# Thirteen clears of a scratch tensor move from SyncE's DMA queue to ScalarE's

## The chip, the core and the metric

The kernel runs on one core of a Trainium2 chip. The metric is device time in microseconds (us) of one execution. The engines of the core are named as in the profile: PE (TensorE, matmuls; PEld are its weight loads), DVE (VectorE), ACT (ScalarE), POOL (GpSimd) and SP (SyncE, which issues transfers here and computes nothing).

## The reference, cut to what matters

Three layers follow each other: attention in which a query sees only the keys of its own cluster, a mixture of eight experts that routes each token to one of them, and a gated feed-forward layer.

```python
q_assign = argmax(einsum('bhsd,hcd->bhsc', q_n, c_n), -1)      # 2 x 8 heads, 768 rows, 64 columns, 16 clusters
k_assign = argmax(einsum('bhsd,hcd->bhsc', k_n, c_n), -1)
mask = q_assign[:, :, :, None] == k_assign[:, :, None, :]
scores = where(mask, scale * q @ k.T, -1e9)
x = softmax(scores) @ v                                        # -> 1536 tokens x 512
expert_idx = argmax(x @ w_gate, axis=1)                        # 8 experts
disp[e, counts[e]] = x[i]                                      # token i to the next free row of its expert
y = relu(disp @ w1) @ w2;  out[i] = gate_w[i] * y[expert, pos] # 512 -> 1024 -> 512
h = out @ w_in;  result = (h * tanh(softplus(h))) @ w_out      # 512 -> 2048 -> 512
```

`disp` starts from zeros; rows that no token takes stay zero.

## The kernel before

The attention is one loop over 32 units (16 heads, two blocks of 384 queries each), each of three steps. In one step PE makes the scores of a pair of key tiles (`s`, L772 and L773), the product whose maximum is wanted (`pm`, L698) and a third of the product with the values (`pa`, L824). ACT takes the exponential (`P`, L780) and copies `pm` out of PSUM (`ev`, L707); DVE halves the copies to a maximum (L714, L718), writes it into the queries' tile (`QX`, L741), makes the low half of the probabilities (`PL`, L796) and normalizes (L847 to L863). The tiles `s`, `pm` and `pl` share a ring of three double banks in PSUM. Per head, `kf`, `qf` and `vf` are loaded (L413), split into high and low halves (`QK`, L528 to L537, copied to `KX` and `QX` at L541 or L544, on ACT or DVE), and turned by transposing transfers: `QKT` (L559), `KXT` and `QXT` (L664), and per unit `Q` (L745). Every one of these transfers is issued from SP.

The rows that the experts read lie in a scratch tensor `xs` in DRAM. It must hold zeros before tokens are written to it. `clear_xs` writes one thirteenth of it from a tile of zeros; the loop's callback `extra` calls it at steps 10, 12, ... 34. After each half of the heads the tokens are routed, and twelve indirect transfers on POOL (`dispatch`, L1171) write them into `xs`; these wait for all clears (`self.CLb`). The transposing transfers `xv` and `xt` (L1442) then read the experts' rows.

The order of all instructions comes from a planner. Each operation is added with an engine and an expected duration and is put into the first gap of that engine's plan in which its inputs are ready and the gap is long enough; `best` takes the engine on which an operation would end first, after a bias. At the end everything is emitted in the order of its planned time, and each engine executes its instructions in that order. Free gaps in PE's plan are filled with matmuls on zeros (L473, L477). For a transfer, `dma` books the issuing queue, a resource `HW` that both hardware queues share, and the transfer time:

```python
hold, hw, delay = (max(1175.0, 348 + xfer), 625, 900) if turn else (475, 450, 1125)
...
t1 = self._gap(q, t, hold)
t = self._gap("HW", t1, hw) if hw else t1
```

In the emitted program each transfer of the hardware queues counts up one of eight completion semaphores, which are taken in turn, and waits until the transfer eight places before it, the last user of that semaphore, has landed.

Of the kernel before, what the change touches and what calls it, by code (L numbers as in the profile page):

```python
# [277 lines left out]
class Builder:  # L278
# [86 lines left out]

    def clear_xs(self, xs, i, n):
        rows = xs.shape[0] // n
        self.nc.sync.dma_start(
            out=xs[i * rows:(i + 1) * rows].rearrange("(a p) c -> p a c", p=128),
            in_=self.zero16.unsqueeze(1).to_broadcast([128, rows // 128, self.RW]))  # L370

# [1809 lines left out]
    def run(self):  # L2181
        tc, nc, E, G, P = self.tc, self.nc, self.E, self.G, self.cfg
        NT, B, NB = self.NT, self.B, self.NB
        profile = [min(a, b) for a, b in zip(P["profile"], self.worst)]
        with ExitStack() as ctx:
            const = ctx.enter_context(tc.tile_pool(name="const", bufs=1))
            dram = ctx.enter_context(tc.tile_pool(name="dram", bufs=1, space=DRAM))
            small = self.small = ctx.enter_context(tc.tile_pool(name="small", bufs=1))
            rows = E * self.slots + max(self.va, default=0)
            xs = dram.tile([-(-rows // (128 * P["zn"])) * 128 * P["zn"], self.RW], F16, name="xs")  # L2190
            idc = dram.tile([self.N, 1], I32, name="idc")
            self.xsave = dram.tile([128, B, NT, 2 * self.KD, 128], F16, name="xsave")
            self.xs_views = dram_disjoint_views(xs[:, :], G)
            idc_views = dram_disjoint_views(idc[:, :], G)
            self.out_views = dram_disjoint_views(self.out, G)
            mkeep = const.tile([128, B * self.H * NB, 3], F32, name="mkeep")
            self.LG = const.tile([128, B, NT, E], F32, name="LG")
            self.OH = const.tile([128, G, E], F16, name="OH")
            self.CS = const.tile([128, B, E], F16, name="CS")
            self.POS = const.tile([128, G], F32, name="POS")  # L2200
            self.OVER = const.tile([128, G], F32, name="OVER")
            self.SLOT = const.tile([128, G], I32, name="SLOT")
            self.prof = const.tile([128, E], F32, name="prof")
            self.many = const.tile([128, B * self.H // self.EG], F32, name="many")
            self.buffers()
            plan = self.new_plan()
            right, actx, rctx, pctx = ExitStack(), ExitStack(), ExitStack(), ExitStack()
            xp = right.enter_context(tc.tile_pool(name="xp", bufs=1, side="right"))
            self.XD = [xp.tile([128, NT, self.XC, 128], F16, name="xd", tag="xd", bufs=B) for b in range(B)]
            self.chp = right.enter_context(tc.tile_pool(name="chp", bufs=1, side="right"))  # L2210

            self.PADb = Buf("pad", 1)

            def extra(z, now):
                k = z - P["zx"]
                if z in (6, 8):
                    pad = self.XD[(z - 6) // 2 % B][:, :, 2 * self.KD].bitcast(F32)
                    plan.op("POOL", 430, lambda: nc.gpsimd.memset(pad, 0.0), add=self.PADb, slack=now)
                if z == 4:
                    self.plan_gate_weights(plan, now)  # L2220
                step, n = P["zs"], P["zn"]
                if 0 <= k < step * n and k % step == 0:
                    assert not self.XSb.writers
                    plan.dma("SP", 22000 / n, lambda: self.clear_xs(xs, k // step, n), add=self.CLb, slack=now)
                if z == 56:
                    plan.dma("SP", 500, lambda: self.clear_idc(idc), new=self.IDCb, slack=now)

            def free(part):
                if part == 1:
                    wo = [xp.tile([128, NT, self.XC, 128], F16, name="xd", tag="xd", bufs=B).rearrange("p t c x -> p (t c x)") for b in range(B)]  # L2230
                    n = self.XC * NT * 128 // (2 * self.DM)
                    return [w[:, f * 2 * self.DM:(f + 1) * 2 * self.DM].rearrange("p (a c) -> p a c", a=2) for w in wo for f in range(n)]

            def before(part):
                if isinstance(part, int):
                    (actx, rctx, pctx)[part].close()
                    return
                use = [u for t in part for b in plan.rings.get(t, ()) for u in b.uses]
                return tuple(max(u[j] for u in use) for j in range(2))

            with tc.manual_schedule():
                self.constants(const, profile)
                self.attention(actx, rctx, pctx, plan, mkeep, extra, self.second_half(plan, profile, xs, idc, idc_views, before, free, mkeep))
                plan.emit()
            self.later.close()
            right.close()
            with tc.If(nc.values_load(self.flag[0:1, 0:1], min_val=0, max_val=1) > 0):
                self.general(mkeep, xs, idc, idc_views, small)
# [125 lines left out]
```

## Time and profile before

| | |
|---|---|
| time, median of 3 runs | 670.84 us (667.78, 670.84, 674.40) |
| profiled execution | 665.95 us |
| its span, first to last instruction | 664.2 us |
| mean granted TensorE clock | 0.99 of full speed |
| stretch in which the 13 clears are issued | 45.6 to 100.6 us |

The span is one execution, the slowest core's (there is one core). Busy times are sums of instruction durations; issues of transfers are not counted in them. A wait is put down to what released it last. "To landing" is the time from a transfer's issue to its completion.

### The profile page before, as it was taken

The page shows a single profiled execution, that of the slowest core. Times are in us where ns is not written, and L with a number is a line of the kernel's source. Part 1 is how long each engine was busy: PE and PEld are TensorE (multiplying, and loading weights), DVE is VectorE, ACT ScalarE, POOL GpSimd, SP SyncE. Part 2 cuts the span into 40 slices and gives each one's busy share as a digit, 9 for nine tenths or more (in the row PEclk, how much of TensorE's full clock was granted, in tenths as well). Part 3 has the DMA queues.
Part 4 walks back from the last instruction along what each step waited for, and adds up shares of the span by engine and source line. Part 5 has one row for each costly group of instructions (what it writes and reads, how often), then busy time and mean ns, then how long its engine had stood idle before and what let it go on. Part 6 is the DMA issues. An engine that isn't in the chain of part 4 may idle for free.

```text
span 664.2 us, 15345 instructions
## 1 busy us (share of the span) xinstructions
PE 626.3 (94%) x6100; PEld 450.7 (68%) x6100; DVE 542.7 (82%) x1047; ACT 487.1 (73%) x738; POOL 67.4 (10%) x113
## 2 busy tenths in 40 slices
PE   7999998799999998999999999979999999999993
PEld 5678776587787896789999886535555555555541
DVE  8999989989998857898899995999798788445542
ACT  6698897688887345576777766998988887666760
POOL 4000111110400030000000000000820000002203
PEclk9999999999998999999999999999999999999998
DMA  9879999894877879998889971213342221000102
GB/s 213 172 144 257 240 249 202 145 176 85 174 150 204 213 269 310 316 288 259 266 256 316 250 267 63 98 63 96 64 63 65 66 93 34 1 0 33 64 1 100
DMA packets 150322, 104.99 MB, mean 158 GB/s; under 512 B 92128, under 2 KB 133088, under 8 KB 150240
## 3 DMA queue, kind: packets, MB, share of 16 engines
q1 hardware_dynamic: 147936, 97.22, 58.8%
q0 software_dynamic: 2304, 6.69, 2.8%
q8 instruction: 50, 0.82, 0.6%
q14 instruction: 32, 0.26, 0.1%
HBM read 68.21 MB, written 14.36 MB: 124 GB/s over the span
## 4 chain that ended last, share of the span: by engine, by line
PE 53%; DVE 16%; DMA 9%; ACT 9%; issue 8%; SPq 2%; POOL 1%; DVEq 0%; POOLq 0%; ACTq 0%
PE fh L1933 13%; PE po L2021 12%; PE py L1648 6%; PE ph L1599 6%; PE pa L824 5%; DVE wh L1481 3%; DMA w2s<-in_moe_w_in_dram 2%; ACT P L780 2%; PE s L772 2%; DVE PL L796 2%; PE s L773 2%; DVE eh L714 2%; ACT ev L707 2%; PE pyv L1774 2%; PE pm L698 2%
## 5 line engine op out<-in xcount | busy, mean ns | idle before, releaser
L2021 PEld LDWEIGHTS <-gt 128*128 128x128 f16 x576 | 56.3, 98 | 64.9
L2021 PE MATMUL po<-xd,gt 128*128 128x512 f16 x432 | 97.3, 379 | 0.0
L780 ACT ACTIVATE P<-s 128x768 f32<-128x768 f32 x96 | 78.1, 814 | 22.1 <-PE s L773 21.5
L1648 PE MATMUL py<-ht,wh 128*128 128x176 f16 (+6 forms) x768 | 79.0, 251 | 0.9 <-DVE wh L1481 0.6
L1599 PE MATMUL ph<-xt,wh 128*128 128x176 f16 (+6 forms) x756 | 76.1, 250 | 3.1 <-DVE wh L1481 2.1
L1933 PE MATMUL fh<-x2l,winh 128*128 128x384 f16 x232 | 75.6, 326 | 2.6 <-DVE x2l L1692 2.6
L1933 PE MATMUL fh<-x2h,winh 128*128 128x384 f16 x232 | 75.6, 326 | 1.6 <-ACT hs L1950 1.6
L1933 PEld LDWEIGHTS <-winh 128*128 128x128 f16 x512 | 50.1, 98 | 38.5 <-issue 2.7
L1933 PE MATMUL fh<-x2h,winl 128*128 128x384 f16 x232 | 75.6, 326 | 0.0
L707 ACT ACTIVATE ev<-pm 128x768 f16<-128x768 f32 x87 | 70.7, 816 | 1.7 <-PE pm L698 1.7
L1599 PEld LDWEIGHTS <-wh 128*128 128x128 f16 x768 | 63.8, 98 | 10.5 <-DVE wh L1481 2.4
L1648 PEld LDWEIGHTS <-wh 128*128 128x128 f16 x768 | 63.6, 98 | 6.4 <-DVE wh L1481 1.3
L772 PE MATMUL s<-Q,KXT 81*128 81x384 f16 x192 | 63.0, 328 | 4.3 <-DMA Q<-QX 3.6
L773 PE MATMUL s<-QKT 128*128 128x384 f16 x192 | 63.0, 328 | 0.0
L796 DVE TENSOR_TENSOR PL<-P 128x768 f16<-128x768 f32 x64 | 60.1, 949 | 0.1
L824 PEld LDWEIGHTS pa<-VW,P 128*128 128x128 f32 x384 | 54.5, 192 | 5.5 <-DVE rpm L1142 0.5
L824 PE MATMUL pa<-VW,P 128*128 128x65 f32 x384 | 55.6, 267 | 0.5 <-DVE rpm L1142 0.5
L698 PE MATMUL pm<-KXT,QXT 80*128 80x384 f16 x192 | 46.4, 327 | 4.8 <-ACT P L780 2.6
L824 PE MATMUL pa<-VX,P 128*128 128x65 f16 x768 | 48.6, 194 | 0.0
L824 PEld LDWEIGHTS <-P 128*128 128x128 bf16 x768 | 47.1, 105 | 0.0
L824 PE MATMUL pa<-VX,PL 128*128 128x65 f16 x384 | 45.3, 192 | 0.0
L1622 ACT ACTIVATE ht<-ph 128x176 f16<-128x176 f32 (+6 forms) x63 | 21.2, 336 | 29.5 <-PE ph L1599 28.0
(284 smaller groups left out, 1268.8 us busy)
## 6 DMA issues: line engine op xcount, KB each, us to landing
w1f<-in_moe_w_dram SPq DMA_DIRECT2D x42, 512.0 KB, 4.8
w2f<-in_moe_w_dram SPq DMA_DIRECT2D x32, 512.0 KB, 5.1
w2s<-in_moe_w_in_dram SPq DMA_DIRECT2D x16, 512.0 KB, 5.3
w2s<-in_moe_w_out_dram SPq DMA_DIRECT2D x16, 512.0 KB, 3.6
xs<-zero SPq DMA_DIRECT2D x13, 576.0 KB, 4.6
xd<-in_moe_w_dram SPq DMA_DIRECT2D x6, 512.0 KB, 4.8
kf<-in_k_dram SPq DMA_DIRECT2D x7, 384.0 KB, 5.3
qf<-in_q_dram SPq DMA_DIRECT2D x7, 384.0 KB, 5.2
```

Of the source, the lines that this page charges most:

```text
L698: nc.tensor.matmul(pm[:, j, 0:384], lhsT=QXT[0:80, g], rhs=KXT[0:80, 3 * j:3 * j + 3].rearrange("c t p -> c (t p)"), start=True, stop=True)
L707: nc.scalar.activation(out=st["ev", u][:, t].rearrange("p (a c) -> p a c", a=2), in_=st["pm", u, t][:, :, 0:384], func=AF.Copy, scale=1.0 ...
L772: nc.tensor.matmul(s[:, j, 0:384], lhsT=KXT[0:81, kt], rhs=Q2[0:81].rearrange("c t p -> c (t p)"), start=True, stop=False)
L773: nc.tensor.matmul(s[:, j, 0:384], lhsT=QKT[:, 1, kt], rhs=QKT[:, 0, 3 * blk:3 * blk + 3].rearrange("c t p -> c (t p)"), start=False, stop ...
L780: nc.scalar.activation(out=st["P32", u, pr], in_=st["s", u, pr][:, :, 0:384], func=AF.Exp, scale=sc)
L796: nc.vector.tensor_tensor(out=st["PL", u][:, 2 * pr:2 * pr + n], in0=st["P32", u, pr][:, 0:n], in1=st["PH", u, pr][:, 0:n], op=ALU.subtract)
L824: nc.tensor.matmul(pa[:, t], lhsT=lhs, rhs=rhs, start=(n == 0), stop=(n == len(mm) - 1))
L1599: nc.tensor.matmul(st["p", i], lhsT=w[:, kk, fs], rhs=xt[:, 2 * kk + a], start=(kk == 0 and n == 0), stop=(kk == KD - 1 and n == 2))
L1622: nc.scalar.activation(out=t[:, 0], in_=st["p", i], func=AF.Relu)
L1648: nc.tensor.matmul(py, lhsT=w[:, f2, dsl], rhs=x, start=(f == 0 and j == 0), stop=(f == NF - 1 and j == 2))
L1933: nc.tensor.matmul(ph[b][:, 0:HB], lhsT=t2[w][:, f, k // 3], rhs=t2["x2"][x][:, k // 3, c0:c0 + HB], start=(k == 0), stop=(k == 3 * KD - 1))
L2021: nc.tensor.matmul(t2["o"][k], lhsT=gt[:, a, ts_], rhs=t2["wo"][f][:, w], start=(first and j == 0), stop=(last and j == 2))
```

## The change

The thirteen clears are issued from ScalarE's hardware queue (`nc.scalar.dma_start`), and the planner books them on ACT instead of on SP. Their size, source, target and the steps at which they are planned stay. All transposing transfers and all loads stay on SyncE's queue. Nothing else is edited; since the planner books another engine, the order that it gives to later operations may differ.

```diff
     def clear_xs(self, xs, i, n):
         rows = xs.shape[0] // n
-        self.nc.sync.dma_start(
+        self.nc.scalar.dma_start(
             out=xs[i * rows:(i + 1) * rows].rearrange("(a p) c -> p a c", p=128),
             in_=self.zero16.unsqueeze(1).to_broadcast([128, rows // 128, self.RW]))
...
                 if 0 <= k < step * n and k % step == 0:
                     assert not self.XSb.writers
-                    plan.dma("SP", 22000 / n, lambda: self.clear_xs(xs, k // step, n), add=self.CLb, slack=now)
+                    plan.dma("ACT", 22000 / n, lambda: self.clear_xs(xs, k // step, n), add=self.CLb, slack=now)
```

## Rows read from the trace of the kernel before

**Rows 1.** Page: busy us (share of the span) x instructions

```profile
PE 626.3 (94%) x6100; PEld 450.7 (68%) x6100; DVE 542.7 (82%) x1047; ACT 487.1 (73%) x738; POOL 67.4 (10%) x113
```

**Rows 2.** Three stretches: length, busy of PE, PEld, DVE, ACT, POOL; clock, DMA share, GB/s

```profile
45.00:101.00 56.00, 54.21 (x726) 42.67 (x723) 52.90 (x123) 50.22 (x88) 4.64 (x5) 1.00 1.03 245
101.00:141.00 40.00, 34.46 (x502) 27.47 (x499) 34.99 (x81) 29.81 (x52) 5.65 (x6) 1.00 1.05 176
141.00:197.00 56.00, 54.95 (x755) 44.34 (x754) 52.80 (x146) 47.30 (x80) 11.06 (x12) 1.00 0.64 138
```

**Rows 3.** PE's first score matmul by line: 45 to 101, 101 to 141, 141 to 197

```profile
L772 PE MATMUL s<-Q,KXT 81*128 81x384 f16 x54 | 17.6, 327 | 0.1
...
L772 PE MATMUL s<-Q,KXT 81*128 81x384 f16 x33 | 10.8, 327 | 2.0 <-DMA Q<-QX 2.0
...
L772 PE MATMUL s<-Q,KXT 81*128 81x384 f16 x56 | 18.3, 326 | 0.1
```

**Rows 4.** PE's waits, 101 to 141: us in total, times, longest us

```profile
PE s L772 <- DMA Q<-QX: 2.0, 1, 2.0
PE pm L698 <- DMA QXT<-QX: 1.6, 1, 1.6
PE pm L698 <- ACT P L780: 1.2, 2, 0.9
```

**Rows 5.** Issues on tile xs: ns min/median/max, first and last start us

```profile
L368 SPq DMA_DIRECT2D xs<-zero x13: 460/572/1054, 45.6 to 100.6; - x13
L1171 POOL DMA_INDIRECT xs<-xd,SLOT x12: 977/978/1528, 169.0 to 242.8; - x12
```

**Rows 6.** SP's timeline, 45 to 101: start us, us of the issue

```profile
46.29 2.47 SPq L745 DMA_TRANSPOSE Q<-QX  x1
...
72.05 1.22 SPq L664 DMA_TRANSPOSE KXT<-KX  x1
...
74.65 0.61 SPq L368 DMA_DIRECT2D xs<-zero  x1
75.31 0.46 SPq L413 DMA_DIRECT2D kf<-in_k_dram  x1
...
80.05 0.94 SPq L368 DMA_DIRECT2D xs<-zero  x1
...
99.28 1.24 SPq L664 DMA_TRANSPOSE QXT<-QX  x1
```

**Rows 7.** SP's waits, 45 to 101: us in total, times, longest us

```profile
SPq L664 <- ACT ev L707: 5.8, 5, 2.0
```

**Rows 8.** DMA issues, 45 to 101, and Q again 141 to 197: KB, median us to landing

```profile
xs<-zero SPq DMA_DIRECT2D x13, 576.0 KB, 4.6
...
Q<-QX SPq DMA_TRANSPOSE x9, 4.8
...
KXT<-KX SPq DMA_TRANSPOSE x4, 4.3
...
Q<-QX SPq DMA_TRANSPOSE x8, 2.4
```

**Rows 9.** ACT's waits, 45 to 101: us in total, times, longest us

```profile
ACT QK L528 <- DMA kf<-in_k_dram: 1.7, 1, 1.7
```

**Rows 10.** ACT's timeline: start us, us

```profile
45.27 0.83 ACT L707 ACTIVATE ev<-pm 128x768 f16<-128x768 f32 x1
45.97 0.40 ACT L860 ACTIVATE xd<-x 128x192 f16<-128x192 f32 x1
```

**Rows 11.** Lines L544, L528, sequencer (ACTq) and ACT, 45 to 101: ns, starts us

```profile
L544 ACTq EVENT_SEMAPHORE  x4: 17/17/38, 49.8 to 92.3; - x4
L544 ACT ACTIVATE KX<-QK x2: 524/534/543, 50.8 to 62.6; 128x384 f16<-128x384 f16 x2
...
L528 ACTq EVENT_SEMAPHORE  x4: 17/17/17, 54.4 to 89.9; - x4
L528 ACT ACTIVATE QK<-kf x4: 508/522/542, 55.6 to 90.0; 128x384 f16<-128x384 f32 x4
```

## Prediction

> **What bounds the kernel now.** I read the busy shares first: PE is busy for 94% of the span, DVE for 82%, ACT for 73% [rows 1]. Such a share mixes stages, so next I cut out the stretch in which the 13 clears are issued, 45 to 101 us, and set two later stretches of the same attention loop beside it [rows 2]. The reader is to see that three engines are nearly full at once there: PE 54.21, DVE 52.90 and ACT 50.22 of 56 us. ACT, which gets the new work, has 56 - 50.22 = 5.8 us free. The DMA share is 1.03 with the clears and 0.64 after them.
>
> Then the pace. Each step of the loop has two matmuls at L772. The stretch with clears holds 54 of them, 27 steps at 2.07 us; 141 to 197 us, without clears, holds 56, 28 steps at 2.00 us [rows 3]. So the clears, where they are now, cost this loop almost nothing. The slow stretch is the one between: 33 matmuls in 40 us, 2.42 us a step, some 6.4 us more than at 2.04 us. In it PE waits 3.6 us for two transposes (2.0 + 1.6) [rows 4], and the last clear has been issued before it begins [rows 5].
>
> **What is removed from SP.** Thirteen issues with a median of 572 ns [rows 5]: 13 x 0.57 = 7.4 us of SP's time. SP's timeline is nearly closed, but what fills it are the issues of 22 transposes, 39.6 us in all (first and last shown) [rows 6], and between and inside them SP waits for others: the longest sum is 5.8 us for ACT at L664 [rows 7]. A queue that waits for its data gains little from a shorter list, so I count the 7.4 us at nothing for the end. What can gain is a transpose that now stands behind a clear: Q lands 4.8 us after its issue in the stretch with clears and 2.4 us after it in the later one [rows 8]. Yet PE hardly waits for transposes while the clears run: its whole idle time there is 56 - 54.21 = 1.8 us [rows 2], and that is the bound of a gain inside the stretch. The largest wait on a DMA there is ACT's for kf, 1.7 us, once [rows 9]; kf is issued at 75.31, right behind the clear of 74.65 [rows 6]. If the late waits of [rows 4] are also a backlog from the clears, 3.6 us come on top: at most 5.4 us to be won.
>
> The bytes do not change: 13 transfers of 576 KB, each landed some 4.6 us after its issue [rows 8]. Here a rule of the Trainium skill speaks against a gain. "DMA: Bandwidth & Descriptors", section "Issuing engines are not separate DMA queues", says that transfers from all issuing engines share the same 16 DMA engines, and that several issuers save only the issue time. By that, the sum is the 7.4 us of SP's time alone, and so nothing where SP waits for others; no run here has yet shown a second hardware queue.
>
> **What is added to ACT.** The trace has no transfer issued from ACT, so its price is bounded by the nearest rows: the same instruction on SP, 0.57 us [rows 5], and from above the indirect transfer on POOL, 0.98 us [rows 5]; from below it is zero, if ACT's datapath works on while its sequencer issues. I take 0.57 us, since form and size are the same; 13 x 0.57 = 7.4 us, with POOL's price 12.7 us. Below zero is excluded for ACT, which gets work and loses none.
>
> How much of it reaches the datapath? ACT's instructions follow each other closely: one that starts at 45.27 and lasts 0.83 us is followed at 45.97, before its end, so the next one already stands ready [rows 10]. How far the sequencer is ahead can be read from the semaphore instructions that it executes itself: the one of L544 runs at 49.8 and its ACTIVATE starts at 50.8, the one of L528 at 54.4 and its ACTIVATE at 55.6 [rows 11]. A lead of 1.0 to 1.2 us covers an issue of 0.57 us. Where there is no lead, the 5.8 us of idle time cover most: 7.4 - 5.8 = 1.6 us are left. I take the middle of 0 and 1.6, +0.8 us. Without either cover it is the full 7.4 us.
>
> A wait moves too. In the program every transfer of the hardware queues counts up one of eight completion semaphores, taken in turn, and waits until the transfer eight places before it has landed. On SP the clears bear this wait; on ACT it would stand before ACTIVATEs, and exp, the copies of pm and so PE's score banks are queued behind it. The closest case I find: the clear at 80.05 has the KXT of 72.05 eight places before it [rows 6]; with the 4.3 us that a KXT takes to land [rows 8] it is there at 76.4, 3.7 us early. A lead of 1.2 us does not use that up: price nothing; if it does, the cover is gone and the next part's price counts.
>
> The clears' reader comes late. The first dispatch on POOL starts at 169.0, and the last clear is issued at 100.6 [rows 5] and landed by some 105. It has over 60 us to spare, whichever queue issues.
>
> **The planner** books 475 ns on ACT instead of on SP for each clear: 6.2 us of ACT's plan. Operations planned later move into other gaps, and some copies (L528, L544) may go to their DVE form. Their order changes, and so does the number of filler matmuls in PE's planned gaps. DVE has 56 - 52.90 = 3.1 us free in the stretch [rows 2]. This can go either way; its size is bounded by the slow stretch, whose PE idle time is 40 - 34.46 = 5.5 us [rows 2]: the order there can hit better or repeat such a hole.
>
> **The sum.** The profiled execution took 665.95 us, 664.2 us of them the span. It lies below all three timed runs and 4.89 us under their median of 670.84 us. A change in the loop's time passes to the end, since the experts start after it, so I add it to the median: 670.84 + 0.8 = 671.6 us. One per cent is 6.7 us, about what a measurement of this kernel can tell from no change.
>
> **Rivals.**
> First, ACT is held, and the kernel is slower. Its place is the clear in ACT's queue while SP is inside the issue of a transpose. SP is in one for 39.6 of 56 us, 71% [rows 6], at a mean of 1.8 us. If two queues cannot issue at once, a clear waits on average for half of one, 0.71 x 0.9 = 0.64 us, and then takes 0.57: 1.21 us, 15.7 us for the 13. Less the idle 5.8 us that is +9.9 us; with the issue alone and none of ACT's idle time usable it is +7.4 us. It decides from the point where ACT's sequencer stands longer than its lead of 1.0 to 1.2 us. The time is 678.2 us, up to 680.7. For it: PE waits for ACT's P at once when ACT is late (1.2 us in [rows 4]), and ACT has the least slack that it ever has. Against it: the lead. The Trainium skill ("Perfetto Trace Analysis", section "DMA Instruction — HWDGE (DVE, Sync)") says that the descriptor generator is shared between two sequencers and locked by the one that uses it. That would make this rival the rule; the trace of a kernel with one such queue cannot show it.
>
> Second, the transposes and loads get past the clears, and the waits of [rows 4] for transposes go: -3.6 us, 667.2 us, at most -5.4, 665.4 us. For it: Q's 4.8 against 2.4 us. Against it: no clear is in flight when those waits occur. "DMA: Bandwidth & Descriptors", section "Queues, rings and completion order", says that SP's and ACT's queues have rings of their own, which each DMA engine serves in turn by packets; by that a Q transpose no longer waits for a whole clear, and this rival's landing times would come true. No row here shows it.
>
> Third, the planner's new order decides, with up to 5.5 us to either side: 665.3 or 676.3 us.
>
> **How the numbers follow.** No change that matters (671.6): 0.50. ACT held (678.2): 0.27. Transposes win (667.2): 0.16. New order: 0.07. Over 677.5 us lie three quarters of the second case and a little of the last, 0.22; under 664.1 us, the other bound, lie a quarter of the third case, some of the last and the scatter of the runs (three lay 6.6 us apart), 0.10; the rest, 0.68, is within 1%. The range goes from a little below the far ends of the winning case and of the new order, 665.4 and 665.3, to just under the far end of the held case: 664 to 680 us.
>
> **What would show it.** Right: ACT gets 13 issues of 0.5 to 0.6 us, its busy time plus idle time in the stretch grows by under 2 us, Q's landing there falls toward 2.4 us, and the pace stays near 2.07 us. Wrong: issues on ACT that last 1 us or more beside SP's transposes, ACT idle time before the ACTIVATE behind a clear, PE waits of several us on ACT's P in the stretch, or a slow stretch that is gone or longer.

## The result and the profile after

The changed kernel takes 672.01 us (median of 20 runs, 667.85 to 681.48), the kernel before 667.21 us (median of 20 runs, 663.31 to 674.40). The ratio is 1.0068 with a 95% interval of 1.0044 to 1.0092: 4.5 us slower, less than one per cent, but not nothing. Here and below the medians are of all runs, while the ratios leave out single runs over 1.5% longer than the fastest of their kernel, so a ratio can differ from the quotient of the medians.

The page of the changed kernel, busy us (share of the span) and instructions, then a row of its part on DMA queues (packets, MB, share of the time of 16 DMA engines), to be read against [rows 1]:

```profile
PE 628.9 (94%) x6097; PEld 452.9 (68%) x6097; DVE 545.0 (82%) x1051; ACT 484.9 (73%) x731; POOL 69.3 (10%) x116
...
q10 hardware_dynamic: 3536, 7.67, 3.3%
```

No engine's busy time has changed by more than 2.6 us. There is now a second hardware queue, q10, and it holds the 13 clears. The span is 668.3 us against 664.2. Three stretches, columns as in [rows 2], and the first score matmul in the first two, as in [rows 3]:

```profile
45.00:101.00 56.00, 50.56 (x646) 40.02 (x644) 49.21 (x115) 42.58 (x71) 5.30 (x7) 0.94 0.91 232
101.00:141.00 40.00, 37.58 (x540) 30.12 (x539) 38.37 (x86) 33.66 (x57) 6.46 (x7) 1.00 0.89 182
141.00:197.00 56.00, 54.49 (x745) 43.67 (x742) 53.23 (x145) 46.26 (x79) 10.45 (x12) 1.00 0.64 137
```

```profile
L772 PE MATMUL s<-Q,KXT 81*128 81x384 f16 x48 | 16.8, 350 | 4.3 <-DVE QK L537 4.3
...
L772 PE MATMUL s<-Q,KXT 81*128 81x384 f16 x37 | 12.1, 326 | 0.1
```

In the stretch with the clears all three engines have lost work: PE 50.56 us against 54.21, ACT 42.58 against 50.22, and 48 matmuls stand where there were 54, three steps. That they all lose says that none of them is the new bound. The slow stretch behind it has become shorter, 37 matmuls in 40 us against 33: two of the three steps come back there. The mean duration in the first row, 350 ns against 327, and the clock of 0.94 say that part of the matmuls ran at the lower clock.

The largest loss has one place. The timeline of SP, ACT and PE around it (start us, us; in brackets the idle time before it):

```profile
59.12 1.23 SPq L664 DMA_TRANSPOSE QXT<-QX  x1
60.45 7.36 SPq L745 DMA_TRANSPOSE Q<-QX  x3
```

```profile
59.74 0.40 ACTq L368 DMA_DIRECT2D xs<-zero  x1
60.11 0.81 ACT L707 ACTIVATE ev<-pm 128x768 f16<-128x768 f32 x1
60.17 0.50 ACTq L368 DMA_DIRECT2D xs<-zero  x1
61.16 0.81 ACT L780 ACTIVATE P<-s 128x768 f32<-128x768 f32 x1 [0.24 <-PE s L773]
61.49 0.64 ACTq L368 DMA_DIRECT2D xs<-zero  x1
...
69.49 0.81 ACT L780 ACTIVATE P<-s 128x768 f32<-128x768 f32 x1 [5.65 <-PE s L773]
```

```profile
68.02 0.48 PE L772 MATMUL s<-Q,KXT 81*128 81x384 f16 x1 [4.27 <-DVE QK L537]
```

ACT issues three clears within 1.8 us, and its ACTIVATEs go on beside the issues. Then PE stands for 4.27 us, and ACT, which waits for PE's scores, for 5.65 us. The name in PE's bracket is the event that came last, not the cause: this score reads the first of the three Q issued from 60.45 on. That transfer has no row of its own for its landing, but the 16 counts of its completion in the trace come between 65.9 and 67.9 us, 7.4 us after its issue; the instruction with which PE waits for that semaphore runs at 67.91, and the score follows at 68.02. The median Q took 4.8 us before [rows 8], though single ones there took up to 7.7 (the Q issued at 104.91 us, behind three loads of 384 KB): a late transpose makes a hole only where PE needs it next. At the same place the kernel before has this order on SP's one line:

```profile
61.72 1.21 SPq L745 DMA_TRANSPOSE Q<-QX  x1
62.97 1.09 SPq L368 DMA_DIRECT2D xs<-zero  x2
64.17 3.01 SPq L745 DMA_TRANSPOSE Q<-QX  x1
67.22 1.05 SPq L368 DMA_DIRECT2D xs<-zero  x1
```

There Q goes first, two clears follow, the next Q, the third clear. The other clears of the changed kernel lie about as far apart as before: two later groups of three take 3.5 and 3.4 us there, 5.4 and 3.0 before, and leave no wait of PE over 1.3 us. What the queues carry from 62 to 64 us shows the difference. First the kernel before, then the changed one (columns as above):

```profile
q1 hardware_dynamic: 951, 0.23, 58.6%
```

```profile
q10 hardware_dynamic: 354, 0.78, 100.9%
q1 hardware_dynamic: 65, 0.01, 2.8%
```

Before, the transposes have the engines to themselves, and the clears wait behind them. After, the clears fill the engines and the transposes get 2.8% of their time. Behind the hole (length, busy of PE and so on, as in [rows 2]):

```profile
64.00:68.00 4.00, 0.00 (x0) 0.01 (x1) 3.90 (x8) 0.00 (x0) 0.99 (x1) 0.97 0.87 251
68.00:75.00 7.00, 6.99 (x36) 4.37 (x37) 2.29 (x8) 4.00 (x7) 0.00 (x0) 0.53 0.95 140
```

PE is idle for the 4 us, and in the 7 us after that the granted clock is 0.53, nearly all of it at the lower of the two levels, 1.2 instead of 2.4 GHz. The first L772 matmul behind the hole, the 43rd, starts 3.6 us later than before, and the 49th, at 75.65 us, where the clock is back, 5.7 us later: the low clock has added 2.0 us. The largest delay is 6.5 us, at the 57th (78.28 us before, 84.73 after). By the 99th it is 2.4 us, by the last 1.7. It grows again to 3.3 us at the experts' first matmul (256.4 before, 259.7 after), and the span ends 4.1 us later. The low clock behind the loop lasts longer in this execution: from 231 to 240 us it is 0.62 on average, 0.81 before. How much of those last 2.4 us that makes I have not separated.

### The profile page after: what moved, and what is told of

It reads as the page before. It is cut to its first block, busy times and chain, and to the rows that moved or that the text cites. A ratio compares the mean times of both kernels' runs of the same rounds, so it can differ in the third digit from the quotient of the medians.

```text
span 668.3 us, 15344 instructions
## 1 busy us (share of the span) xinstructions
PE 628.9 (94%) x6097; PEld 452.9 (68%) x6097; DVE 545.0 (82%) x1051; ACT 484.9 (73%) x731; POOL 69.3 (10%) x116
## 4 chain that ended last, share of the span: by engine, by line
PE 47%; DVE 25%; issue 9%; DMA 7%; ACT 6%; SPq 2%; POOL 2%; DVEq 0%; POOLq 0%; ACTq 0%
PE fh L1933 13%; PE po L2021 12%; PE py L1648 6%; PE ph L1599 6%; DVE PL L796 4%; PE pa L824 4%; DVE eh L714 4%; DVE wh L1481 3%; DMA w2s<-in_moe_w_in_dram 2%; DVE mkeep L718 2%; PE s L772 2%; PE s L773 2%; POOL out_dram L2050 1%; DVE QK L537 1%; DMA xs<-xd,SLOT 1%
## 5 line engine op out<-in xcount | busy, mean ns | idle before, releaser
L772 PE MATMUL s<-Q,KXT 81*128 81x384 f16 x192 | 63.8, 332 | 7.2 <-DVE QK L537 4.3
L2065 POOL DMA_INDIRECT idc<-ids,ci x12 | 18.3, 1526 | 226.5 <-DVE ci L1369 223.2
```

The source lines that it names most:

```text
L772: nc.tensor.matmul(s[:, j, 0:384], lhsT=KXT[0:81, kt], rhs=Q2[0:81].rearrange("c t p -> c (t p)"), start=True, stop=False)
```

## The experiments

Three theories. **Theory 1**: on a queue of their own the clears are no longer spaced by SP's line, since ACT comes to their issue early; they go out early, close together and beside the transposes, which land late. In later expectations it is theory A, and "only the bunching hurts" is B. **Theory 2**: the planner's new order costs the time. **Theory 3**: ACT pays for the issues, by their length, by a wait for SP or by the completion semaphores. For delays I give the start of the n-th L772 matmul against that of before; they are of one execution each, and executions of one program lie over 10 us apart, so the ratios decide and the traces say where. In this section, "before" is the kernel before run on the same chip.

**The queue alone.** Before's plan and order to the letter, only the issuing engine changed:

```diff
-        self.nc.sync.dma_start(
+        self.nc.scalar.dma_start(
             out=xs[i * rows:(i + 1) * rows]...
```

> The planner books the clears on SP as before, so PE, DVE and ACT keep the order of the kernel before; only the queue that issues the clears is ScalarE's. Theory 1 (beside clears of a second queue, which come in bursts of three because ScalarE's sequencer runs ahead, the Q transposes land later, and PE stands): slower than before by 3 to 6 us, with a hole of some 4 us in PE near 65 us. Theory 2 (the planner's new order costs the time: six copies of L860 go to DVE, and PE waits for DVE): within 1.5 us of before and no hole. Theory 3 (ScalarE is held by its issues): slower by 5 us or more, with idle time of ACT behind the issues.

671.38 us against 669.29, ratio 1.0048 (1.0016 to 1.0079). The hole has moved to another bunch. SP's timeline, ACT's, and the first matmul after the hole:

```profile
86.86 3.45 SPq L664 DMA_TRANSPOSE QXT<-QX  x1
```

```profile
87.86 2.37 ACTq L368 DMA_DIRECT2D xs<-zero  x2
```

```profile
94.68 0.66 PE L698 MATMUL pm<-KXT,QXT 80*128 80x384 f16 x2 [2.67 <-DMA QXT<-QX]
```

Three clears leave at 86.1, 87.9 and 88.3 us; the QXT issued at 86.86 lands after 7.8 us and PE waits 2.67 us for it, here under the right name. Against before, whose plan this is, the first twelve clears leave 0.4 to 4.0 us sooner. How close they lie doesn't decide alone: the closest three, at 62.24 to 63.46 us, leave no wait over 0.7 us, since the Q that is needed first went out ahead of them, at 61.62, and landed after 4.0 us, while the Q issued among them took 8.5. The stretch from 95 to 101 us then runs at a clock of 0.50. The delay is 1.7 us at the 57th matmul, 6.0 at the 75th, 2.3 at the 99th. The queue is enough to make the loss; the new order isn't needed.

**The order alone.** The changed kernel's plan, but the clears issued from SP:

```diff
-        self.nc.scalar.dma_start(
+        self.nc.sync.dma_start(
```

> The order of the changed kernel on PE, DVE and ACT, but the clears issued from SyncE's queue. Theory 1 (the second queue delays the transposes): back to the kernel before, within 1.5 us, no hole in PE near 65 us. Theory 2 (the new order costs the time): as slow as the changed kernel, 4 to 5 us over before, with the hole. Theory 3 (ScalarE held): as before.

668.88 us against 669.29, ratio 0.9992 (0.9964 to 1.0020). Windows of 45 to 101 and 101 to 141 us:

```profile
45.00:101.00 56.00, 52.98 (x706) 42.61 (x705) 54.21 (x125) 47.64 (x80) 6.50 (x8) 1.00 1.03 247
101.00:141.00 40.00, 37.67 (x550) 30.34 (x547) 38.51 (x87) 33.16 (x57) 5.65 (x6) 1.00 0.94 180
```

The clock is 1.00 in both: no hole has lowered it. Theory 2 falls as the cause of the loss.

**Clears farther apart, on ACT's queue and on SP's.** A clear every fourth step instead of every second, to some 153 us, once in the changed kernel and once in the kernel before:

```diff
-    zs=2, zn=13, rest=300, ...
+    zs=4, zn=13, rest=300, ...
```

On ACT's queue: 

> The changed kernel with a clear at every fourth step instead of every second, so that no three clears are in flight at once; they end by some 150 us, before the first dispatch at 170. Theory 1 (bursts of clears delay the Q transposes): the hole near 65 us goes, time within 1.5 us of before or better. Theory 2 (order): depends on the new order alone; the planner moves three more splits to DVE, so 2 to 5 us slower than before.

On SP's queue: 

> Before with a clear every fourth step instead of every second, on SP's queue (control for the clears spread the same way on ACT's queue, 671.6 us). All theories: the same as before within 1.5 us in the stretch with clears; if spreading helps the slow stretch behind it, up to 3 us faster; if the clears that now end at 153 us meet the first loads of weights, up to 2 us slower.

On ACT's queue 671.61 us against 669.29, ratio 1.0009 (0.9976 to 1.0041); on SP's 668.54 us against 667.29, 1.0012 (0.9977 to 1.0046). The issues from 45 to 101 us, median us to landing, on ACT's queue and on SP's:

```profile
xs<-zero ACTq DMA_DIRECT2D x7, 576.0 KB, 4.9
...
Q<-QX SPq DMA_TRANSPOSE x9, 3.3
QXT<-QX SPq DMA_TRANSPOSE x5, 5.2
```

```profile
xs<-zero SPq DMA_DIRECT2D x7, 576.0 KB, 4.5
...
Q<-QX SPq DMA_TRANSPOSE x10, 4.0
QXT<-QX SPq DMA_TRANSPOSE x5, 2.8
```

Spaced out, the same 13 issues on ACT cost nothing that can be measured; by the interval it is at most 2.7 us. Q lands a little sooner than beside clears on SP, QXT later (5.2 us against 2.8). So the issues aren't the price of the changed kernel, whose interval (1.0044 to 1.0092) lies above this one, and spacing helps. That it takes the second queue's part away entirely isn't shown, and the planner's order differs here too. The profiled execution on ACT's queue has a 3.31 us wait for a Q at 205.9 us, long after the last clear: holes of this size occur in this loop without clears too.

**Without a reservation on ACT.** In the changed kernel the planner books 1 ns of ACT for a clear:

```diff
+        if q == "ACT":
+            hold = 1
```

> The changed kernel, but the planner books 1 ns instead of 475 ns on ACT for a clear, since the trace shows ACTIVATEs that run on beside the issue. Its plan is as long as before's (0.1 us shorter). Theory 1 (second queue delays transposes): still slower than before by 3 to 6 us with a hole. Theory 2 (order made by the booked time): within 1.5 us of before.

674.75 us, ratio 1.0091 (1.0060 to 1.0122). A third order, and clears in a bunch again (60.6, 61.1 and 62.3 us). Its one profiled execution, 666.75 us, is the fastest of its ten runs and shows a wait of 1.94 us behind that bunch (again under DVE's name; the Q issued at 61.03 lands at 66.40, the score follows at 66.53), with a clock of 0.52 in the 7 us after it. The loop is 4.3 us late at the 57th matmul and level with before at the 99th, so this execution doesn't say where the 5 us and more of the timed runs go. The booked time on ACT isn't what costs.

**Every second clear.** Before's plan; six clears from ACT, seven from SP:

```diff
-        self.nc.sync.dma_start(
+        (self.nc.sync, self.nc.scalar)[i % 2].dma_start(
```

> Before's plan and order; every second clear (6 of 13) is issued from ACT's queue, 7 stay on SP's. Theory 1 (clears of a queue of their own run ahead, lie close together and hold up the transposes beside them): some bunching is left, since ACT's clears are no longer in line with SP's, but only in pairs: +1 to +3 us against before, less than the +2.1 us to +4.5 us that all 13 on ACT gave; Q and QXT land within 6 us. Theory 3 (ACT pays for each issue): 6 x 0.4 to 0.6 us, +2 to +4 us, ACT's idle time up, no hole of PE behind a transpose. If the plan alone were the cause: no change.

670.13 us against 667.29, ratio 1.0029 (0.9998 to 1.0060): between the two, but its interval just touches 1, so it decides little. PE's waits from 40 to 141 us (in total, times, longest):

```profile
PE pm L698 <- DMA QXT<-QX: 3.9, 2, 2.5
PE s L772 <- DMA Q<-QX: 2.8, 2, 2.1
```

Both are for transposes, as theory 1 has it; ACT accounts for 0.4 us. The size of the waits is above what I expected of pairs.

**The issues without the bytes.** Before, with its clears on SP, and beside each an 8 KB transfer from ACT into a spare tensor (line numbers are one higher in this kernel):

```diff
+        self.nc.scalar.dma_start(out=self.spare[i * 128:(i + 1) * 128], in_=self.zero16[:, 0:32])
```

> Before with its 13 clears on SP, and beside each clear a transfer of 8 KB of zeros into a spare tensor issued from ACT's queue. So ACT's queue has 13 issues as in the changed kernel, but no bytes to speak of. Theory 1: the same as before within 1.5 us, no hole in PE's work, issues on ACT of 0.4 to 0.6 us. Theory 3 (the issue itself, or a generator that the two queues share, costs time on ACT): +3 us or more, with ACT idle ahead of ACTIVATEs behind the issues.

669.48 us against 667.29, ratio 1.0027 (0.9995 to 1.0060). Neither theory's number: the interval just reaches below 1, and the medians lie 2.2 us apart, less than the 3 us of theory 3. The transposes land as before (Q 5.0 us, QXT 2.9, medians from 45 to 101 us), so issues on a second queue without the bytes don't hold them up. Where time may go, the trace shows. SP's and ACT's timelines:

```profile
49.11 1.77 SPq L414 DMA_DIRECT2D kf<-in_k_dram  x1
```

```profile
54.32 0.34 ACTq L371 DMA_DIRECT2D spare<-zero  x1
54.71 0.81 ACT L708 ACTIVATE ev<-pm 128x768 f16<-128x768 f32 x1 [3.22 <-DMA kf<-in_k_dram]
```

The issue itself takes 0.34 us. But ACT stands for 3.22 us before it, until the kf issued at 49.11 has landed at 54.30. A copy of `pm` has nothing to do with kf; the transfer before it has, since it takes the completion semaphore that kf holds. This is the wait on a semaphore eight places back, and behind it the ACTIVATEs stand in line. It happened once here, with 26 transfers where the changed kernel has 13, and PE then stood 2.0 us for that copy. In the changed kernel one clear did wait so (that of 51.00 us, for the QXT of 43.90, which landed at 50.98), but ACT had work meanwhile, and the ACTIVATE directly behind a clear waits nowhere longer than 0.24 us, so this is not what it pays.

**On POOL's queue.** Nothing stands ahead of the first clears on POOL. Once with the planner booking POOL (both edits), and once with before's plan and only the issuing engine changed (the first edit):

```diff
-        self.nc.sync.dma_start(
+        self.nc.gpsimd.dma_start(
...
-                    plan.dma("SP", 22000 / n, ...
+                    plan.dma("POOL", 22000 / n, ...
```

Booked on POOL: 

> Clears issued and booked on POOL's queue instead of ACT's; SP's transposes as in the changed kernel. Theory 1: what matters is that the clears leave SP's line, not that ACT issues them; POOL is nearly idle here, so the clears can run ahead still more and meet the transposes: +1 to +6 us, Q's or QXT's landing at 7 us or more somewhere and a wait of PE of over 2 us behind it. Theory 3: ACT is free of issues, so no change against before (within 1.5 us). POOL's issue takes 1 us or so, which hides.

Before's plan: 

> Before's plan and order to the letter, but the clears issued from POOL, where nothing stands ahead of them, so they go out at 7 to 22 us. Theory A: the first transposes starve beside them, some 15 to 20 us of wait for one QKT, and the end is 12 to 20 us later, as where POOL was planned too. In the stretch that then has no clears (45 to 169 us) the loop runs at 2.0 us a step: against before 6 to 9 us are won back there. If it was the planner's order on POOL's version that did that, the stretch shows the slow steps of before again.

685.66 us against 667.29, ratio 1.0283 (1.0233 to 1.0333), and 681.05 against 669.55, 1.0182 (1.0142 to 1.0222). The first kernel: all clears (issues on POOL), SP's timeline, PE's, and the queues from 24 to 32 us:

```profile
L368 POOL DMA_DIRECT2D xs<-zero x13: 725/725/934, 7.6 to 21.9; - x13
```

```profile
10.64 9.62 SPq L559 DMA_TRANSPOSE QKT<-QK  x1
...
21.85 13.95 SPq L559 DMA_TRANSPOSE QKT<-QK  x1
```

```profile
36.14 0.81 PE L607 MATMUL pl<-CT,QKT 128*128 128x16 f16 x24 [20.05 <-DMA QKT<-QK]
```

```profile
q0 software_dynamic: 666, 2.74, 97.4%
q1 hardware_dynamic: 665, 0.17, 9.4%
```

This is theory 1 at full size, three times the most that I expected of it: the clears, planned for 45 to 101 us, all leave in the first 22 us. SP's issue of a QKT, 1.4 to 1.8 us at 55.9 and 67.9 us of the changed kernel, lasts 9.62 and 13.95 us, and PE waits 20.05 us for one QKT. The two queues take turns packet for packet, 666 to 665, but a packet of the clears holds 4.1 KB and one of the transposes 0.26 KB, so the transposes get 6% of the bytes. ACT issues nothing here, so theory 3 has no part in it. In the second kernel I was wrong about the place: only seven clears leave from 7.6 us on, with 9.5 us of wait for a QKT; six stand on POOL behind additions (L863) that wait for the loop, and leave at 82 to 112 us. With those six in it the stretch that I wanted free of clears wins nothing back: its 60 matmuls of L772 from the 39th to the 99th take 66.4 us, before 66.5.

The first kernel bears on what the clears cost the kernel before. There the same 60 matmuls, without clears, take 59.4 us, 7.1 us less than before. Of these, 3.4 us lie up to the 75th matmul, among the clears (35.6 us, 39.0 before; the order alone, with nine clears there, 39.5). The other 3.7 us lie behind it, in the slow stretch (23.8 us, 27.5 before), and no clear has to go for them: the order alone, with its clears where before has them, takes 24.1 us there. Each figure is of one execution.

**Bunches of three.** Three clears every sixth step in place of one every second, booked on SP in both kernels; the second issues them from ACT (the last edit is its alone):

```diff
-                if 0 <= k < step * n and k % step == 0:
-                    plan.dma("SP", 22000 / n, lambda: self.clear_xs(xs, k // step, n), ...
+                for i in range(n):
+                    if k == i // 3 * 3 * step:
+                        plan.dma("SP", 22000 / n, lambda i=i: self.clear_xs(xs, i, n), ...
...
-        self.nc.sync.dma_start(
+        self.nc.scalar.dma_start(
```

From SP: 

> Clears in bunches of three (every sixth step instead of one every second), all on SP's queue, planned there. Control for the next kernel. Theory A (it is the second queue that hurts: clears of another queue go on beside a transpose and it lands late): in one line a bunch delays only what stands behind it, by three landings at most, some 4 us, and the transposes that matter are issued again at once: +0 to +3 us against before. Theory B (only the bunching hurts, whichever queue issues): +3 to +6 us, with holes of PE behind the bunches as in the changed kernel, and the next kernel the same within 2 us.

From ACT: 

> The kernel with bunches of three, same plan and order, but the clears issued from ACT's queue. Theory A: slower than the bunches on SP by 3 us or more, a transpose beside each bunch lands after 7 us or later, several holes of PE of 2 us and more, and low clock behind them. Theory B: the same as the bunches on SP within 2 us. If the queues' sharing helped the transposes (they would not stand behind the bunch): faster than the bunches on SP by 2 us or more, with Q's landing at 3 us.

From SP 672.00 us, from ACT 674.57, against 669.55: ratios 1.0057 (1.0030 to 1.0085) and 1.0093 (1.0061 to 1.0125). The transposes' landings from 45 to 101 us with clears from SP, then with clears from ACT, and there PE's largest wait in that stretch:

```profile
Q<-QX SPq DMA_TRANSPOSE x9, 4.9
...
QXT<-QX SPq DMA_TRANSPOSE x5, 2.8
```

```profile
Q<-QX SPq DMA_TRANSPOSE x9, 5.9
QXT<-QX SPq DMA_TRANSPOSE x4, 7.1
```

```profile
PE pm L698 <- DMA QXT<-QX: 5.6, 2, 4.1
```

Bunching costs by itself, on SP's line too, though its execution shows no wait of PE over 1.2 us from 40 to 141 us. On ACT's queue QXT needs 7.1 us in place of 2.8 and PE waits 5.6 us for it, from SP not at all; the loop's delay at its last matmul is 7.4 us against 1.8. SP's timeline around the largest hole, with clears from SP, then ACT's and SP's with clears from ACT:

```profile
88.59 2.40 SPq L664 DMA_TRANSPOSE QXT<-QX  x1
91.03 2.23 SPq L368 DMA_DIRECT2D xs<-zero  x3
```

```profile
89.09 0.43 ACTq L368 DMA_DIRECT2D xs<-zero  x1
89.67 0.38 ACTq L368 DMA_DIRECT2D xs<-zero  x1
...
89.86 2.99 SPq L664 DMA_TRANSPOSE QXT<-QX  x1
```

SP's bunches are as close as ACT's or closer (three starts within 1.1 us, ACT's within 1.0 to 4.4), but on SP's line this QXT goes ahead of the bunch and lands after 4.0 us. From ACT two clears leave ahead of it, and it lands after 9.8 us. The plan is the same, so what the second queue adds here is that clears get past a transpose. In the timed runs it adds 2.6 us: set directly against each other, the means of the 9 and 12 runs differ by 2.7 us, with a 95% interval of 0.8 to 4.6. That it adds something is shown; how the rest of the loss divides isn't settled.

**Smaller clears on SP.** 26 of half the size, one every second step, to 153 us:

```diff
-    zs=2, zn=13, rest=300, ...
+    zs=2, zn=26, rest=300, ...
```

> 26 clears of half the size on SP's queue, one every second step (to some 153 us). Theory A: less stands in line ahead of a transpose at once, so Q lands sooner (3 to 4 us instead of 4.8 in 45 to 101 us) and up to 3 us are won in the loop; twice the issues cost SP 7.4 us, which hide: 0 to -3 us against before. If SP's time is what is short: +1 to +4 us.

668.21 us against 669.55, ratio 0.9991 (0.9961 to 1.0022): no measurable difference. The window of 45 to 101 us, as above:

```profile
45.00:101.00 56.00, 55.78 (x774) 45.36 (x772) 54.76 (x135) 52.93 (x93) 0.00 (x0) 1.00 0.89 201
```

PE's 1.8 us of idle time in this stretch fall to 0.2, Q lands after 3.5 us, and at the 99th matmul the loop is 4.8 us ahead. At the last it is 1.9 us ahead, and the span is 664.1 us, that of before. The loop's gain was lost again by its end and behind it, and none of the thirteen kernels is shown to be faster than the one before.

## Why the prediction was right, and where it was not

That the time lies 0.4 us from the forecast is luck: two misses cancel. I added 0.8 us to a median of three runs, 670.84; the median of 20 is 667.21, and the effect is 4.5 us. The forecast that nothing over 1% happens holds; the term that should give its size doesn't. Of its own signs of being right, two failed: Q's landing rose to 5.3 us in place of falling toward 2.4, and the pace in the stretch went from 2.07 us a step to 2.33 (24 steps in 56 us). No sign of an ACT that is held came.

**What is added to ACT** was priced at 0.57 us an issue. In the trace it is 0.38 (13 issues, 378/379/639 ns), and the ACTIVATEs run on. It is covered as forecast, though the lead of 1.0 to 1.2 us was read from two pairs: the eight pairs of semaphore and ACTIVATE at L544 and L528 in that stretch [rows 11] give 0.1 to 2.2 us. The 0.8 us are nothing that shows: clears farther apart on the same queue cost nothing measurable. The first rival, ACT held, is refuted: the ACTIVATEs directly behind the issues wait 0.24 us at most. The Trainium skill ("Perfetto Trace Analysis", section "DMA Instruction — HWDGE (DVE, Sync)") has a lock on a shared descriptor generator. Single issues on ACT did last 1.91 us (the queue alone) and 1.41 us (bunches), both beside an issue of a QXT on SP that itself lasted 3.45 and 2.99 us and for which PE then waited. Whether such a lock or the full DMA engines held these issues no run here shows; ACT was not what PE waited for.

**The completion semaphores** were priced at nothing, and that holds in the changed kernel. But the 3.7 us of reserve were not to be had: one clear there did wait, and the 8 KB kernel shows how thin the cover is, 3.22 us of ACT once, with 13 more transfers in turn.

**What is removed from SP** holds the step that failed: "What can gain is a transpose that now stands behind a clear". I took the queue to be only a delay, so that its removal could gain but not lose. The queue was also what kept the transposes ahead of the clears, and the clears apart: three clears needed 4.2 us on SP's line (62.97 to 67.22) with a Q between them, and 1.8 us on ACT. The second rival, transposes past the clears, thus ran the other way: Q in 45 to 101 us went from a median of 4.8 us to 5.3, QXT from 3.1 to 7.1. In the profiled execution the term that stands in place of the 0.8 is one hole of some 4 us and the 2.0 us of its low clock; 6.5 us late at most, the loop wins some 4 us back up to the 99th matmul.

The Trainium skill's rule of rings served in turn by packets ("DMA: Bandwidth & Descriptors", section "Queues, rings and completion order"), by which that rival's landings would come true, doesn't carry it. The POOL kernel agrees with the rule, 666 packets to 665, and shows what it makes of the bytes: they go to the queue with the large packets. In the changed kernel from 61 to 68 us the clears' queue moved 816 packets with 1.77 MB and SP's 1239 with 0.29 MB: 2.2 KB against 0.23 KB a packet. In the 2 us shown above the turns weren't even there, 65 packets to 354, and why is open. Against the section "Issuing engines are not separate DMA queues" of the same page of the Trainium skill, by which another issuer saves only its issue time, the runs show a loss: 2.1 us between the medians for ACT and 11.5 us for POOL, with before's plan in both.

**The planner** was given up to 5.5 us; its order by itself measured 0.9992.

**The pace.** "The clears ... cost this loop almost nothing" was read from 2.07 against 2.00 us a step inside the stretch [rows 3]. From the 39th to the 75th matmul they cost some 3.4 us by the POOL kernel (18 steps, 2.16 against 1.98 us). The note that the waits of [rows 4] may be a backlog of the clears is not borne out: the order alone is 3.4 us faster than before in the slow stretch too, and has the clears. The Q for which PE waits 2.0 us, at 123.3 us of the kernel before, left SP right behind four other transposes, and landed after 2.3 us; the last clear had landed at 104.5:

```profile
114.70 6.13 SPq L1018 DMA_TRANSPOSE XT<-xd  x4
120.93 1.20 SPq L745 DMA_TRANSPOSE Q<-QX  x1
```

**A change in the loop's time** does not simply pass to the end, as the sum had it: a loop that was 1.9 us ahead ended with the same span, and one that was 1.7 us late ended 4.1 us late.

## What to carry to other kernels

A transfer that stands in line with others is spaced and ordered by them. Before moving a bulk transfer to a free queue, ask what will hold it back there: the emptier the queue's engine, the earlier the transfers leave (ACT +0.5%, POOL +1.8% to 2.8%), and the transposes that they get ahead of pay. If a second queue is wanted, space the bulk transfers by hand, which left no measurable loss here, and check the landing of the small ones, not the issuing engine's time.

## What the runs showed of the hardware

- Transposes starve beside large transfers of another queue: two QKT took 25.5 and 16.5 us to land in the POOL kernel, the same two 3.8 and 6.6 us before, and SP's own issue lasted up to 13.95 us, so everything behind it on SP stood too.
- Two queues with work in hand took turns packet for packet in the POOL kernel, 666 to 665 from 24 to 32 us, and so 2.74 to 0.17 MB.
- A hole of 4.3 us in PE's work was followed by 7 us at a granted clock of 0.53, which added 2.0 us, about half of the hole again.
- An issue of a 576 KB transfer on ACT takes 0.38 us, less than the 0.57 us on SP [rows 5], and ACT's datapath works on meanwhile.
